# Attention plus rational feed-forward on one core: in the first part's units ScalarE forms the numerator's first step ahead of the absolute value

## The chip, the core and the metric

The program runs on one core of one Trainium2 chip, in float32 from end to end. The metric is the device time of one execution in microseconds (us). The kernel before was run three times: 1244.38, 1244.65 and 1247.54 us, so the median is 1244.65. The engines are named as the profile names them: PE (TensorE's matmuls), PEld (its weight loads), ACT (ScalarE), DVE (VectorE), POOL (GpSimd) and SP (SyncE, whose queue issues most DMAs).

## The reference

Block-causal attention, then a feed-forward layer with a rational function between its two products:

```
scores = (q @ k.T) / 8, masked by 64 x 64 blocks        # 8 x 8 heads, 576 tokens, head size 64
x = softmax(scores) @ v                                  # 4608 x 512
h = x @ w_in                                             # 4608 x 2048
P = a0 + a1*h + a2*h*h + a3*h*h*h
Q = 1 + |b0|*|h| + |b1|*h*h
out = (P / (Q + 1e-6)) @ w_out                           # 4608 x 512
```

## The kernel before

**Attention** runs over 32 pairs of heads, p0 to p31. For each pair, PE makes transposes of q and k (`tp`), scores (`s`), transposes of the exponentials (`t`) and the product with v (`o31_0`, `o31_1` for pair 31). ACT makes the exponentials (L560) and the high halves of split numbers (`ptrh`, `xh`), DVE the maxima (L548) and the low halves (`ptrl`, L612), POOL scales the exponentials (L572). The result goes to the DRAM scratch `xscr`.

**The feed-forward layer** needs each float32 product as three passes over high and low halves. It has two parts. Part 0 (`ph == 0`) covers the first 10 of 16 blocks of the hidden size for 14 chunks of 256 tokens. It runs between the attention pairs, and fills PE's time there. Part 1 covers what is left, after the attention, in chunks of 512 tokens. A unit of part 0 is two hidden blocks by 256 tokens, five units a chunk, 70 in all. A tile's name gives part, chunk and unit: `h0_10_1` is the hidden tile of part 0, chunk 10, unit 1. Its steps are:

- `first`: 24 matmuls of 256 columns make `h` in PSUM (L229). Then ACT reads `h` for `u = |h|` (L236) and for `s = a3*h + a2` (L238), and makes `v = b1*u + b0` (L239). POOL makes `u = v*u` (L243). DVE makes `s = s*h` (L244) and `s = (s + a1)*h` (L245), which also read `h` in PSUM.
- `recip`: ACT makes Ln (L251), Exp (L258) and `s + a0` (L259). DVE makes `gh` (L260) and a correction (L261), POOL the remainder (L263).
- `split`: POOL makes `gl`, the low half (L275).
- `second`: 12 matmuls of 512 columns take `gh` and `gl` with `w_out` (L299). The passes over `gh` can start before `gl` is there.

There is one PSUM tile for `h` in part 0, so the next unit's first matmul waits for L245 of this unit. `u`, `v` and `s` have two buffers each.

**The order on the engines** is not the order of the code. The lines name the work and its dependences, and a scheduler places the instructions by its own estimate of when each could run (`schedule_with_timeline_sim=True`, in the launch code). So moving one line can move others, on every engine. Part 0's units come into the code's order a step at a time between attention steps, by a fixed table of goals, which the change does not touch.

Of the kernel before, what the change touches and what calls it, by code (L numbers as in the profile page):

```python
# [12 lines left out]
AF = mybir.ActivationFunctionType  # L13
# [60 lines left out]
def attn_ffn_kernel(  # L74
# [11 lines left out]
    nc = tc.nc  # L86
# [97 lines left out]
    class Ffn:  # L184
# [34 lines left out]
        def first(self, ph, c, u):  # L219
            xs = self.x[ph, c]  # L220
            tag = f"{ph}_{c}_{u}"
            pool = self.pools[self.n % len(self.pools)]
            hp = self.hpools[self.n % len(self.hpools)]
            h = hp.tile([128, NBU[ph], CTS[ph]], F32, name=f"h{tag}", tag="a", bufs=1 if hp is ps_h else 3)
            for j in range(NBU[ph]):
                w, f = self.block(ph, c, NBU[ph] * u + j)
                for dc in range(4):
                    for i, (y, hl) in enumerate(((0, 1), (0, 0), (1, 0))):
                        nc.tensor.matmul(h[:, j, :], lhsT=w.win(f, dc, y), rhs=xs[dc][:, hl, :],  # L229
                                         start=(dc == 0 and i == 0), stop=(dc == 3 and i == 2))  # L230
            self.n += 1
            hf = h.rearrange("p j t -> p (j t)")
            ut = pool.tile([128, 512], F32, name=f"u{tag}", tag="u", bufs=CBUFS if pool is ffn else 2)
            vt = pool.tile([128, 512], F32, name=f"v{tag}", tag="v", bufs=CBUFS if pool is ffn else 2)
            st = pool.tile([128, 512], F32, name=f"s{tag}", tag="s", bufs=CBUFS if pool is ffn else 2)
            nc.scalar.activation(out=ut, in_=hf, func=AF.Abs)  # L236
            if ph == 0:
                nc.scalar.activation(out=st, in_=hf, func=AF.Identity, scale=a3, bias=a2)  # L238
                nc.scalar.activation(out=vt, in_=ut, func=AF.Identity, scale=b1, bias=b0)  # L239
            else:  # L240
                nc.scalar.activation(out=st, in_=hf, func=AF.Identity, scale=na3, bias=na2)  # L241
                nc.gpsimd.tensor_scalar(out=vt, in0=ut, scalar1=b1, scalar2=b0, op0=ALU.mult, op1=ALU.add)  # L242
            nc.gpsimd.tensor_tensor(out=ut, in0=vt, in1=ut, op=ALU.mult)  # L243
            nc.vector.tensor_tensor(out=st, in0=st, in1=hf, op=ALU.mult)  # L244
            nc.vector.scalar_tensor_tensor(out=st, in0=st, scalar=a1, in1=hf,  # L245
                                           op0=ALU.add if ph == 0 else ALU.subtract, op1=ALU.mult)
            self.m[ph, c, u] = (pool, ut, vt, st)
# [114 lines left out]
    with ExitStack() as actx:  # L362
# [61 lines left out]
        def behind(ins, first):  # L424
            tc.add_manual_dep(ins.ins, first.ins.name,
                              mybir.DependencyInfo(mybir.DependencyClass.NoSync, mybir.DependencyReason.DATA),
                              reason="order")
# [367 lines left out]
```

## Time and profile before

| what | us |
|---|---|
| three runs, median | 1244.65 |
| the profiled execution, its own time | 1246.05 |
| its span in the trace | 1244.3 |
| PE busy in the span | 1191.3 |
| DVE, ACT, POOL busy in the span | 921.3, 908.5, 876.7 |
| the stretch 100 to 850 us (attention and part 0 together): PE busy | 721.85 of 750 |
| the stretch 850 to 1244 us (part 1 alone): PE busy | 388.92 of 394 |

The profiled execution took 1.4 us more than the median, and 1.75 us of its time lie outside the span. A window's row gives each engine's busy time in a stretch. What is missing from the stretch is that engine's idle time. The wait rows then say what PE waited for. Matmuls overlap, so the distance from one start to the next, and not a matmul's own length, is what it costs PE.

### The profile page before, as it was taken

What the parts mean: (1) busy time and instruction counts of PE and PEld (TensorE: products, weight loads), DVE (VectorE), ACT (ScalarE), POOL (GpSimd) and SP (SyncE); (2) the same over time, 40 slices, a digit from 0 to 9 for tenths busy, and PEclk for the clock granted to TensorE, in tenths of its full rate; (3) what the DMA queues carried; (4) which work ended last, traced back from release to release, by engine and by line L of the source; (5) the groups of instructions that cost most, each with busy time, mean ns of one, the idle gap of its engine ahead of it and who ended that gap; (6) DMA issues with size and microseconds to landing.
All of it is one profiled execution on the core that took longest, in us unless ns stands there. A gap on an engine that the chain in (4) does not pass through costs nothing.

```text
span 1244.3 us, 21931 instructions
## 1 busy us (share of the span) xinstructions
PE 1191.3 (96%) x7124; PEld 1008.8 (81%) x7124; DVE 921.3 (74%) x2016; ACT 908.5 (73%) x2025; POOL 876.7 (70%) x1043
## 2 busy tenths in 40 slices
PE   6888999999999999999999999999999999999998
PEld 4666888888888878888888888878888888888886
DVE  6878888777888777877777777647666766677764
ACT  6877888877988878888888888756555655555554
POOL 4666778877888877787777877756665656665664
PEclk8999999999999999999999999999999999999999
DMA  8782344463544545443333342444014344443100
GB/s 233 208 232 71 94 138 113 121 179 89 143 114 132 132 125 143 108 136 100 100 103 92 105 110 68 113 154 189 1 64 131 120 136 136 136 136 102 43 1 34
DMA packets 199506, 145.67 MB, mean 117 GB/s; under 512 B 136288, under 2 KB 164960, under 8 KB 199392
## 3 DMA queue, kind: packets, MB, share of 16 engines
q1 hardware_dynamic: 196624, 143.15, 40.1%
q10 hardware_dynamic: 2704, 1.11, 0.3%
q8 instruction: 57, 0.93, 0.3%
q14 instruction: 57, 0.47, 0.1%
q0 software_dynamic: 64, 0.00, 0.0%
HBM read 92.28 MB, written 41.94 MB: 108 GB/s over the span
## 4 chain that ended last, share of the span: by engine, by line
PE 71%; ACT 8%; POOL 7%; DVE 5%; DMA 5%; issue 3%; SPq 1%; POOLq 0%; ACTq 0%; DVEq 0%
PE h L229 28%; PE o L299 26%; PE o L664 5%; PE t L598 4%; PE s L530 4%; ACT p L560 2%; PE o L625 2%; POOL gl L275 2%; DMA xt<-xh 1%; POOL u L263 1%; PE tp L438 1%; POOL p L572 1%; PE s L513 1%; DMA wri<-in_moe_w_in_dram 1%; DMA x<-xscr 1%
## 5 line engine op out<-in xcount | busy, mean ns | idle before, releaser
L229 PE MATMUL h<-x,wpi 128*128 128x256 f32 (+1 forms) x2568 | 453.6, 324 | 7.2 <-DMA x<-xscr 2.5
L229 PEld LDWEIGHTS h<-x,wpi 128*128 128x128 f32 x2568 | 380.7, 190 | 53.0 <-issue 6.0
L299 PE MATMUL o<-wpo,gh 128*128 128x512 f32 x1152 | 343.8, 395 | 0.0
L299 PEld LDWEIGHTS o<-wpo,gh 128*128 128x128 f32 x1152 | 212.8, 188 | 43.3 <-issue 0.7
L299 PE MATMUL o<-wpo,gl 128*128 128x512 f32 x576 | 210.3, 400 | 8.6 <-POOL gl L275 8.2
L572 POOL TENSOR_SCALAR p<-p,rc 128x128 f32<-128x128 f32 (+4 forms) x288 | 176.1, 623 | 48.4 <-DVE rc L569 32.9
L243 POOL TENSOR_TENSOR u<-v,u 128x512 f32<-128x512 f32 x144 | 187.5, 1302 | 13.2 <-ACT v L239 5.4
L560 ACT ACTIVATE p<-s,nm 128x288 f32<-128x288 f32 (+4 forms) x320 | 168.3, 534 | 25.2 <-DVE nm L548 19.9
L251 ACT ACTIVATE v<-u,qcb 128x512 f32<-128x512 f32 x144 | 105.1, 730 | 82.0 <-POOL u L243 81.7
L244 DVE TENSOR_TENSOR s<-s,h 128x512 f32<-128x512 f32 x144 | 98.5, 684 | 86.4 <-ACT s L241 65.2
L236 ACT ACTIVATE u<-h 128x512 f32<-128x512 f32 x144 | 86.4, 600 | 102.3 <-PE h L229 96.2
L548 DVE TENSOR_REDUCE nm<-s 128x1 f32<-128x128 f32 (+4 forms) x288 | 129.4, 474 | 7.4 <-PE s L513 4.7
L278 POOL TENSOR_TENSOR gl<-s,gh 128x512 fp32r<-128x512 f32 x74 | 95.8, 1294 | 55.0 <-ACT gh L277 54.9
L598 PE MATMUL t<-ident,p 128*128 128x128 f32 x800 | 122.5, 279 | 8.6 <-POOL p L572 4.1
L299 PEld LDWEIGHTS o<-wpo,gl 128*128 128x128 f32 x576 | 104.7, 189 | 31.1 <-POOL gl L275 12.4
L611 ACT CAST ptrh<-t 128x512 fp32r<-128x512 f32 (+1 forms) x189 | 98.4, 542 | 36.9 <-PE t L598 36.6
L612 DVE TENSOR_TENSOR ptrl<-t,ptrh 128x512 fp32r<-128x512 f32 (+1 forms) x189 | 115.5, 627 | 11.5 <-ACT ptrh L611 10.4
L242 POOL TENSOR_SCALAR v<-u,bab 128x512 f32<-128x512 f32 x74 | 57.2, 774 | 91.0 <-ACT u L236 90.9
L598 PEld LDWEIGHTS t<-ident,p 128*128 128x128 f32 x800 | 91.0, 141 | 27.8 <-POOL p L572 6.8
L263 POOL TENSOR_TENSOR u<-s,u 128x512 f32<-128x512 f32 x70 | 90.3, 1290 | 30.3 <-DVE u L261 16.2
L245 DVE SCALAR_TENSOR_TENSOR s<-s,coef,h 128x512 f32<-128x512 f32 x144 | 106.2, 738 | 2.4
L530 PE MATMUL s<-k,q 64*128 64x512 f32 (+3 forms) x768 | 86.4, 343 | 6.6 <-ACT p L560 2.9
(110 smaller groups left out, 2031.5 us busy)
## 6 DMA issues: line engine op xcount, KB each, us to landing
x<-xscr SPq DMA_DIRECT2D x44, 256.0 KB, 4.0
xscr<-xl SPq DMA_DIRECT2D x32, 288.0 KB, 2.4
out_dram<-os SPq DMA_DIRECT2D x34, 256.0 KB, 3.3
qr<-in_q_dram SPq DMA_DIRECT2D x64, 128.0 KB, 2.8
kr<-in_k_dram SPq DMA_DIRECT2D x62, 128.0 KB, 2.5
xt<-xh SPq DMA_DIRECT2D x54, 144.0 KB, 2.3
xscr<-xh SPq DMA_DIRECT2D x54, 144.0 KB, 2.5
pscr<-os SPq DMA_DIRECT2D x14, 512.0 KB, 2.7
```

The source lines that it names most:

```text
L229: nc.tensor.matmul(h[:, j, :], lhsT=w.win(f, dc, y), rhs=xs[dc][:, hl, :], start=(dc == 0 and i == 0), stop=(dc == 3 and i == 2))
L243: nc.gpsimd.tensor_tensor(out=ut, in0=vt, in1=ut, op=ALU.mult)
L245: nc.vector.scalar_tensor_tensor(out=st, in0=st, scalar=a1, in1=hf, op0=ALU.add if ph == 0 else ALU.subtract, op1=ALU.mult)
L251: nc.scalar.activation(out=vt, in_=ut, func=AF.Ln, bias=qcb)
L263: nc.gpsimd.tensor_tensor(out=ut, in0=st, in1=ut, op=ALU.subtract)
L299: nc.tensor.matmul(self.o[m], lhsT=g[:, j, ms], rhs=w.wout(f, y), start=(u == 0 and j == 0 and i == 0), stop=(u == nu - 1 and j == NBU[ph] ...
L530: mm = nc.tensor.matmul(s["s", t, h], lhsT=q[hs, x, 128 * t:128 * t + 128], rhs=k[hs, y, 0:128 * (t + 1)], start=(n == 0 and t == i), stop ...
L548: nc.vector.reduce_max(out=nm[:, j:j + 1], in_=s[d, j][:, :w] if i == 4 else s["s", i, j], axis=AX.X, negate=True)
L560: nc.scalar.activation(out=dst, in_=s.pop((d, j2))[:, :w] if i == 4 else s.pop(("s", i, j2)), func=AF.Exp, bias=nm[:, n:n + 1], scale=1.0, ...
L572: nc.gpsimd.tensor_scalar(out=x, in0=x, scalar1=rc[:, j2:j2 + 1], scalar2=1.0, op0=ALU.mult, op1=ALU.mult)
L598: nc.tensor.transpose(ps[:, 128 * x:128 * x + 128], src[:, 128 * kb:128 * kb + 128], ident)
L612: nc.vector.tensor_tensor(out=dl, in0=src, in1=dh.bitcast(F32), op=ALU.subtract)
```

## The change

In part 0, ACT now makes `s` from `h` first and `u = |h|` after it, then `v` as before. In part 1 nothing moves. No operation is added or taken away, and no shape or buffer changes.

```diff
-            nc.scalar.activation(out=ut, in_=hf, func=AF.Abs)
+            if ph:
+                nc.scalar.activation(out=ut, in_=hf, func=AF.Abs)
             if ph == 0:
                 nc.scalar.activation(out=st, in_=hf, func=AF.Identity, scale=a3, bias=a2)
+                nc.scalar.activation(out=ut, in_=hf, func=AF.Abs)
                 nc.scalar.activation(out=vt, in_=ut, func=AF.Identity, scale=b1, bias=b0)
```

In the changed kernel the three ACT lines are L239 (`s`), L240 (`u`) and L241 (`v`), and every line behind them is two higher (L299 is L301).

In the built programs, the wait of DVE's product (L244, then L246) on ACT is for L238 in all 70 units before, and for L240 in all 70 units now. Each is the second of ACT's two reads of `h`. So the product waits for both reads in either program.

The scheduler's order differs on all engines from the first unit of part 0 to the last. PE's order is the same up to unit 0_0_0's second products, and again from the last attention pair's end on, that is for all of part 1.

**ACT, unit 0_3_1.** Before, from its absolute value on; `p` are exponentials of attention, `ptrh` high halves of transposes:

```order
L236 ACTIVATE u0_3_1_4301<-h0_3_1_4276 128x512
L238 ACTIVATE s0_3_1_4303<-h0_3_1_4276,coef_97 128x512
L560 ACTIVATE p1_124,sm11_4_3605<-s11_4_1_3607,nm11_4_3604 128x256
L560 ACTIVATE p1_124,sm11_4_3605<-s11_4_0_3606,nm11_4_3604 128x256
L239 ACTIVATE v0_3_1_4302<-u0_3_1_4301,bab_102 128x512
L611 CAST ptrh_1534<-t11_1_0_3652 128x4x128
L611 CAST ptrh_1534<-t11_1_1_3659 128x4x128
```

The same unit now, from its first ACT operation on:

```order
L239 ACTIVATE s0_3_1_4303<-h0_3_1_4276,coef_97 128x512
L240 ACTIVATE u0_3_1_4301<-h0_3_1_4276 128x512
L562 ACTIVATE p3_126,sm12_1_3749<-s12_1_1_3751,nm12_1_3748 128x512
L562 ACTIVATE p3_126,sm12_1_3749<-s12_1_0_3750,nm12_1_3748 128x512
L613 CAST ptrh_1534<-t11_3_0_3786 128x2x2x128
L241 ACTIVATE v0_3_1_4302<-u0_3_1_4301,bab_102 128x512
```

`s` and `u` have changed places, `v` stands one row further behind the first of them, and the unit as a whole stands later beside the attention (pair 12's exponentials, no longer pair 11's). Over the 70 units, `v` stands 2.7 rows behind the first operation before and 3.5 now, and the Exp 11.6 and 11.8 rows. An Abs is followed at once by its own `v` in 4 units before and in 23 now, a Ln by its own Exp in 12 and in 22.

**PE, unit 0_3_1's second products.** Before, from pair 13's transposes to unit 0_3_1's first pass over `gl`:

```order
L438 MATMUL tp13_0_3795<-ident_92,qr13_3674 128x128 x4
L299 MATMUL o0_3_0_4679<-wpo0_2_0_1161,gh0_3_1_4509 128x512 x2
L299 MATMUL o0_3_1_4680<-wpo0_2_0_1161,gh0_3_1_4509 128x512 x2
L299 MATMUL o0_3_0_4679<-wpo0_2_0_1161,gl0_3_1_4510 128x512
L530 MATMUL s12_2_1_3813<-k12_3413,q12_3412 128x384
```

The same place now, from behind its passes over `gh` on:

```order
L229 MATMUL h0_3_3_4586<-x0_3_0_4001,wpi0_6_0_1349 128x256 x6
L229 MATMUL h0_3_3_4586<-x0_3_1_4004,wpi0_6_2_1377 128x256 x5
L532 MATMUL s12_4_1_3990<-k12_3413,q12_3412 128x256
L532 MATMUL s12_4_0_3989<-k12_3413,q12_3412 128x256
L532 MATMUL s12_4_1_3990<-k12_3413,q12_3412 128x256
L532 MATMUL s12_4_0_3989<-k12_3413,q12_3412 128x256
L532 MATMUL s12_4_1_3990<-k12_3413,q12_3412 128x256
L532 MATMUL s12_4_0_3989<-k12_3413,q12_3412 128x256
L229 MATMUL h0_3_3_4586<-x0_3_1_4004,wpi0_6_2_1377 128x256
L229 MATMUL h0_3_3_4586<-x0_3_0_4001,wpi0_6_0_1349 128x256 x6
L229 MATMUL h0_3_3_4586<-x0_3_1_4004,wpi0_6_2_1377 128x256 x6
L301 MATMUL o0_3_0_4679<-wpo0_2_0_1161,gl0_3_1_4510 128x512
```

Unit 0_3_3's whole first product and a set of scores now stand between the passes over `gh` and the pass over `gl`, where nothing stood before.

**PE, the end of unit 0_10_1's first product.** Before, from its last rows to the scores of pair 26 (`o0_9_0` and `o0_9_1` are second products of chunk 9):

```order
L229 MATMUL h0_10_1_9539<-x0_10_1_9230,wpi0_2_2_1133 128x256 x4
L299 MATMUL o0_9_0_9175<-wpo0_8_0_1594,gl0_9_4_9484 128x512
L299 MATMUL o0_9_1_9176<-wpo0_8_0_1594,gl0_9_4_9484 128x512
L299 MATMUL o0_9_0_9175<-wpo0_9_0_1621,gh0_9_4_9483 128x512 x2
L598 MATMUL t25_1_1_9158<-ident_92,p3_126 128x128 x4
L513 MATMUL s26_0_0_9210<-k26_8907,qtl0_121 128x288 x3
L299 MATMUL o0_9_0_9175<-wpo0_9_0_1621,gl0_9_4_9484 128x512
L299 MATMUL o0_9_1_9176<-wpo0_9_0_1621,gh0_9_4_9483 128x512 x2
L299 MATMUL o0_9_1_9176<-wpo0_9_0_1621,gl0_9_4_9484 128x512
```

Now, from the same tile's last rows on:

```order
L600 MATMUL t25_1_1_9158<-ident_92,p3_126 128x128 x4
L515 MATMUL s26_0_0_9210<-k26_8907,qtl0_121 128x288 x3
L229 MATMUL h0_10_1_9539<-x0_10_1_9230,wpi0_2_2_1133 128x256 x3
L301 MATMUL o0_9_1_9176<-wpo0_9_0_1621,gh0_9_4_9483 128x512
L301 MATMUL o0_9_1_9176<-wpo0_9_0_1621,gl0_9_4_9484 128x512
L301 MATMUL o0_10_0_9912<-wpo0_0_0_736,gh0_10_0_9612 128x512 x2
```

Six of chunk 9's eight second products, four transposes and three score matmuls stand ahead of the first product's end now; before they stood behind it.

At the end of the attention, four second products of unit 0_13_1 that stood ahead of pair 31's last product with v stand behind it now.

## Rows read from the trace of the kernel before

**Rows 1.** The page's first part: busy time of each engine, its share of the span, and instructions.

```profile
PE 1191.3 (96%) x7124; PEld 1008.8 (81%) x7124; DVE 921.3 (74%) x2016; ACT 908.5 (73%) x2025; POOL 876.7 (70%) x1043
```

**Rows 2.** Windows of the span: from:to and length in us, then busy us (and instructions) of PE, PEld, DVE, ACT and POOL, the granted TensorE clock as a share of full speed, the DMA share and GB/s. The whole stretch of attention and part 0, the stretch of part 1, a 100 us piece of part 1, then twelve pieces of 50 us.

```profile
100.00:850.00 750.00, 721.85 (x4930) 627.65 (x4927) 583.69 (x1408) 612.92 (x1457) 580.49 (x717) 1.00 0.44 120
850.00:1244.00 394.00, 388.92 (x1716) 321.70 (x1714) 263.87 (x389) 220.01 (x359) 238.53 (x214) 1.00 0.26 86
900.00:1000.00 100.00, 100.00 (x443) 82.81 (x442) 68.45 (x103) 57.92 (x95) 61.35 (x55) 1.00 0.33 108
200.00:250.00 50.00, 49.78 (x344) 43.19 (x343) 37.83 (x94) 42.26 (x100) 40.25 (x50) 1.00 0.42 112
250.00:300.00 50.00, 45.94 (x311) 39.66 (x310) 38.45 (x96) 39.26 (x97) 36.71 (x46) 0.97 0.47 130
300.00:350.00 50.00, 49.56 (x349) 43.20 (x349) 42.17 (x102) 44.27 (x106) 40.16 (x52) 1.00 0.50 137
350.00:400.00 50.00, 48.38 (x348) 42.82 (x347) 40.99 (x104) 42.92 (x103) 41.43 (x50) 1.00 0.51 137
400.00:450.00 50.00, 47.57 (x320) 41.50 (x320) 39.75 (x93) 39.16 (x94) 39.80 (x50) 0.97 0.45 125
450.00:500.00 50.00, 47.55 (x333) 40.67 (x331) 38.99 (x99) 41.12 (x103) 39.14 (x49) 1.00 0.47 127
500.00:550.00 50.00, 48.62 (x340) 42.79 (x338) 42.32 (x104) 43.55 (x106) 39.08 (x49) 1.00 0.46 128
550.00:600.00 50.00, 47.60 (x331) 42.09 (x332) 37.65 (x92) 40.25 (x96) 40.30 (x49) 1.00 0.41 106
600.00:650.00 50.00, 49.86 (x351) 43.70 (x351) 38.84 (x97) 40.52 (x100) 39.08 (x49) 1.00 0.38 96
650.00:700.00 50.00, 49.19 (x349) 43.47 (x348) 37.22 (x96) 41.70 (x102) 38.51 (x51) 1.00 0.41 105
700.00:750.00 50.00, 50.00 (x347) 44.11 (x346) 38.27 (x96) 43.11 (x103) 38.58 (x49) 1.00 0.38 104
750.00:800.00 50.00, 49.19 (x344) 42.90 (x342) 35.66 (x92) 38.64 (x92) 37.62 (x48) 1.00 0.34 92
```

**Rows 3.** What PE waited for between 100 and 850 us: us in total, times, longest us.

```profile
PE o L299 <- POOL gl L275: 8.2, 11, 1.8
PE o L648 <- DVE ptrl L612: 2.3, 2, 1.6
PE h L229 <- DVE s L245: 2.2, 4, 1.0
...
PE h L229 <- DVE rc L569: 1.6, 1, 1.6
```

**Rows 4.** ACT and DVE in order of time at unit 0_0_1: start us, length us, instruction, and the idle time before it with what ended it. Then two ACT rows at 337 us, a Ln and the Exp that needs it.

```profile
123.92 0.60 ACT L236 ACTIVATE u<-h 128x512 f32<-128x512 f32 x1 [0.94 <-PE h L229]
124.41 0.77 ACT L238 ACTIVATE s<-h,coef 128x512 f32<-128x512 f32 x1
125.08 0.81 ACT L239 ACTIVATE v<-u,bab 128x512 f32<-128x512 f32 x1
...
125.22 0.69 DVE L244 TENSOR_TENSOR s<-s,h 128x512 f32<-128x512 f32 x1 [1.69 <-ACT s L238]
...
337.08 0.72 ACT L251 ACTIVATE v<-u,qcb 128x512 f32<-128x512 f32 x1
337.83 0.63 ACT L258 ACTIVATE v<-v 128x512 f32<-128x512 f32 x1
```

**Rows 5.** PE and POOL in order of time around unit 0_3_1's `gl`, then three windows there.

```profile
276.88 0.62 PE L229 MATMUL h<-x,wpi 128*128 128x256 f32 x3
...
288.61 1.27 POOL L275 TENSOR_TENSOR gl<-u,v 128x512 fp32r<-128x512 f32 x1
...
289.93 0.49 PE L299 MATMUL o<-wpo,gl 128*128 128x512 f32 x1 [1.79 <-POOL gl L275]
...
288.00:291.00 3.00, 1.21 (x12) 0.83 (x11) 3.00 (x6) 3.00 (x8) 2.92 (x3) 1.00 0.38 87
291.00:294.40 3.40, 3.40 (x15) 2.60 (x12) 2.81 (x9) 2.51 (x6) 1.86 (x4) 0.50 0.01 2
294.40:298.00 3.60, 3.60 (x31) 3.50 (x30) 3.60 (x10) 3.28 (x12) 2.48 (x4) 1.00 0.17 38
```

**Rows 6.** Two windows at 440 us.

```profile
437.70:441.10 3.40, 1.85 (x14) 1.11 (x11) 2.81 (x9) 3.40 (x9) 3.15 (x5) 1.00 0.00 0
441.10:444.60 3.50, 3.50 (x19) 3.50 (x18) 3.46 (x10) 3.50 (x10) 1.64 (x4) 0.51 0.49 176
```

**Rows 7.** PE and POOL in order of time for unit 0_10_1: the end of its first product, its `gl` made, its first passes over `gl`. The row at 546 us is a run of 14 matmuls of 256 columns, and the one behind it starts where the run ends.

```profile
648.67 0.72 PE L229 MATMUL h<-x,wpi 128*128 128x256 f32 x4
...
661.81 1.28 POOL L275 TENSOR_TENSOR gl<-u,v 128x512 fp32r<-128x512 f32 x1
...
664.29 0.72 PE L299 MATMUL o<-wpo,gl 128*128 128x512 f32 x2
...
546.10 1.83 PE L229 MATMUL h<-x,wpi 128*128 128x256 f32 x14
547.77 0.60 PE L598 MATMUL t<-ident,p 128*128 128x128 f32 x4
```

**Rows 8.** PE where part 1's first product goes on, behind the end of the attention.

```profile
837.61 0.70 PE L229 MATMUL h<-x,wpi 128*128 128x512 f32 x2 [1.36 <-DMA x<-xscr]
```

## The prediction

> **What bounds the kernel now.** I read the page's shares first, then the windows, then what PE waited for, and then single places in order of time. PE is busy for 1191.3 of 1244.3 us, and no other engine for more than 921.3 [rows 1]. The windows split the span in two [rows 2]. From 850 us on, in part 1, 443 matmuls of 512 columns fill 100 us with no idle time: one each 0.226 us, at a granted clock of 1.00. That part is as fast as its matmuls. Between 100 and 850 us, where part 0 runs between the attention's pairs, PE is idle for 750 - 721.85 = 28.15 us. This is all that an order can win there, short of the smaller gaps that the windows count as busy. PE's longest waits there are for `gl` from POOL: 8.2 us in 11 times. Behind them come 2.3, 2.2 and a row of still smaller ones, of many kinds [rows 3]. So the kernel is bound by PE, and its losses are many short waits, none on one place alone.
>
> A long wait has a second price. After the 1.79 us that PE waits for `gl` at 288 to 290 us, the granted clock is 0.50 (1.2 in place of 2.4 GHz) for 3.4 us, with 15 matmuls in 3.4 us, and behind that 31 in 3.6 us at 1.00 [rows 5]. At 437.7 to 441.1 us PE is idle for 3.40 - 1.85 = 1.55 us, and the clock then is 0.51 for 3.5 us [rows 6]. Each such stretch loses about half of itself, 1.7 us. Shorter waits are followed by no such stretch: pieces with 2.4 us of idle time in all stay at 1.00 [rows 2].
>
> **The change, part by part.** Part 1 keeps its order: 0 us.
>
> *The first product's chain.* The words of the change suggest that DVE's product `s*h` starts earlier, by one Abs. It doesn't, since the built program has it wait for the second of ACT's two reads of `h`, whichever that is. In the trace the Abs starts at 123.92, the Identity for `s` at 124.41, and DVE's product at 125.22, which is 1.30 us after the first of the two [rows 4]. Now the Identity comes first. Its follower starts 125.08 - 124.41 = 0.67 us after it, the Abs takes 0.60, and DVE starts some 0.04 later as before: 1.31 us. So the PSUM tile of `h` is free no earlier, and the 2.2 us for which PE waits on L245 [rows 3] stay: 0 us.
>
> The trace shows no kernel in which a product starts after the Identity alone. The Trainium skill's page "PSUM — Partial Sum Buffer", section "PSUM bank collisions raise a hardware error", says that the compiler's scheduler orders any two instructions of different engines that touch one bank and quadrant, reads of ACT and DVE included. That is a rule against a gain from this change, and the built waits agree with it. Without it the product would start some 0.6 us earlier, and the 2.2 us could go, by which the time would be 1242.4.
>
> *ACT's own time.* The three operations keep their lengths. But two neighbours on ACT that don't need each other overlap: 0.60 long, 0.49 from start to start. Where the second needs the first, as the Exp the Ln, it starts 0.03 us after its end [rows 4]. The difference is 0.14 us. Now 23 - 4 = 19 more units have the Abs straight ahead of its `v`, and 22 - 12 = 10 more a Ln straight ahead of its Exp. So ACT is held for 29 x 0.14 = 4.1 us more, against 750 - 612.92 = 137 us of idle time in the stretch [rows 2]. The cover is large: 0 us on the path. Without it, the 4.1 us would be the price.
>
> *When `gl` is made.* Chain: `v` is later by the 0.14 and by the 0.8 rows that it stands further back. One ACT instruction holds its queue for 612.92 / 1457 = 0.42 us on the average [rows 2], so together some 0.5 us. The Exp, which `gh` and so `gl` need, is only 0.2 rows further back: 0.1 us, or 0.2 with its own dependence. I take 0.3, between the ends 0.1 and 0.5. Way: I priced PE's rows between a unit's last first product and its first pass over `gl`, for all 70 units, at 0.226 us for 512 columns and (547.77 - 546.10) / 14 = 0.119 for 256 [rows 2, 7], the other shapes in proportion. This estimate gives 14.3 us as the mean before and 14.5 now, so 0.2 of the 0.3 is given back. The 11 waits for `gl` [rows 3] grow by 11 x 0.1 = 1.1 us. This is the middle of a wide interval, because single places move far more than the mean. Two of them:
>
> - Unit 0_3_1: its first product ends at 276.88 + 3 x 0.119 = 277.24, its `gl` is made at 288.61 + 1.27 = 289.88, and PE stood there from 288.14 on [rows 5]. Now 24 matmuls of 256 columns, 24 x 0.119 = 2.9 us, lie between. This wait of 1.79 us should go, and the 1.7 us of slow clock behind it too.
> - Unit 0_10_1: its first product ends at 648.67 + 4 x 0.119 = 649.15, `gl` is made at 663.09, and PE comes for it at 664.29, with 1.2 us to spare [rows 7]. Now six matmuls of 512 columns and seven short ones have moved to the other side: 6 x 0.226 + 7 x 0.119 = 2.2 us. PE comes 1.0 us too early.
>
> Bounds of the term: if all waits for `gl` go, -8.2. If each unit's `gl` came as long after its first product as before, while PE came by the new order, 16 units would wait for 18.7 us in all by the same estimate, which is 18.7 - 8.2 = +10.5. I don't take that end. A unit whose passes the scheduler puts earlier is mostly one whose chain it sees end earlier.
>
> *The attention's end.* PE waits 1.36 us for part 1's inputs at 837.61 [rows 8], which come from the last pair's output. Four second products, 4 x 0.226 = 0.9 us, now stand behind that pair. This fills 0.9 of the wait: -0.9 us, between 0 and -1.36.
>
> *The rest of the order.* Transposes, scores and second products change places all over the stretch, and SP's loads with them. The PE waits other than for `gl` have no reason to grow or to shrink: the same instructions, the same lengths, another draw. What a draw is worth is to be read from the windows. PE's idle time in the twelve pieces from 200 to 800 us is 16.8 us, from 0.00 to 4.06, with a mean of 1.40 and a standard deviation of 1.24 us. For 15 such pieces a draw strays by 1.24 x 3.9 = 4.8 us. To that come the stretches at half clock. There are two now, and none to four would be -3.4 to +3.4 us.
>
> Sum: 0 + 0 + 0 + 1.1 - 0.9 + 0 = +0.2 us. The profiled execution took 1246.05, with 1.75 us outside its span, and it would become 1246.25. It is 1.4 above the median, so the median to expect is 1244.65 + 0.2, about 1244.9.
>
> **The rivals.**
> - *Faster, chance 0.23.* The long waits of the old order go and the new one has only short ones, so that the clock stays at 1.00. For it: the place at 288 us gets 2.9 us of cover, and ten of the fifteen units that PE caught without `gl` have a longer way now. Price: 1.79 + 1.55 us of waits and 2 x 1.7 of clock, 6.7 us, which gives 1238. Against it: a new order has long waits of its own. It decides from the point at which no new wait reaches about 1.5 us.
> - *Slower, chance 0.31.* `gl` becomes a wait at places like unit 0_10_1. By the estimate eleven units that had time to spare lose more of their way than they had, and a later `v` adds up to 0.5 us to each. Price: half of the +10.5, 5.3 us, and one stretch more at half clock, 1.7: 7 us, which gives 1251.7. It decides once `gl` comes later than PE by more than 8.2 us in sum. Against it: the mean way has grown.
> - *The change doesn't do what it says*, in that DVE starts no earlier. That is what I expect, and the forecast has it in it. If DVE did start by 0.6 us earlier, the price is the 2.2 us above, and it would still be within 0.3%.
>
> **How the numbers follow.** The forecast, no difference, is the likeliest: 0.46. A measurement of this kernel can tell about 0.3% from no change, 3.7 us, so "within" is 1240.9 to 1248.4. The draw's 4.8 us and some 1.7 for the clock make 5.1 us; 8 times in 10 is 1.28 x 5.1 = 6.5 us to each side, 1238.4 to 1251.4. To take in more of the bounds of the `gl` term, of which the one above is the further, I widen it to 1237 to 1255. Faster by over 0.3% has 0.23, slower by over 0.3% 0.31: the sum of chain and waits leans a little to the slow side.
>
> **What would show it right or wrong.** In the profile after: part 1 still 443 matmuls in 100 us; DVE's product released by the Abs (L240) and starting 1.3 us after the Identity's start; no wait for `gl` and no half clock after unit 0_3_1; a wait of about 1 us for `gl` at unit 0_10_1; waits for `gl` of 7 to 12 us in all; the idle time of PE between 100 and 850 us within some 5 us of 28.15; a wait of some 0.5 us for part 1's inputs. It would be wrong if idle time moved by more than the draw, or if the waits for attention's tiles (`p`, `ptrl`) moved with a sign of their own, for which I have found no reason.

## The result, and the profile after

The new kernel takes 1259.4 us (median of four runs, 1257.93 to 1259.92), the kernel before 1244.99 on the same chip (1244.38 to 1247.54). The ratio is 1.0094, interval 1.0072 to 1.0117: slower by 14.4 us. The prediction had 1244.9 and a range up to 1255. The profiled execution took 1259.8, its span is 1258.0, 13.7 more than before. Line numbers behind L236 are two higher than before: `s` is L239, `u` L240, `gl` L277, the exponentials L562.

The page's first part answers to [rows 1], the windows to [rows 2]:

```profile
PE 1196.4 (95%) x7124; PEld 1010.9 (80%) x7124; DVE 930.8 (74%) x2016; ACT 910.0 (72%) x2025; POOL 871.6 (69%) x1043
```

```profile
100.00:850.00 750.00, 713.77 (x4897) 620.78 (x4898) 585.34 (x1399) 606.81 (x1446) 566.76 (x711) 1.00 0.42 114
900.00:1000.00 100.00, 100.00 (x443) 82.77 (x443) 67.66 (x101) 57.72 (x95) 61.12 (x56) 1.00 0.30 98
200.00:250.00 50.00, 46.56 (x329) 40.77 (x328) 38.70 (x102) 42.47 (x104) 38.28 (x51) 1.00 0.46 126
250.00:300.00 50.00, 49.00 (x338) 42.63 (x338) 40.21 (x97) 41.87 (x103) 40.79 (x52) 1.00 0.46 128
300.00:350.00 50.00, 46.84 (x329) 40.67 (x328) 40.25 (x95) 40.24 (x100) 35.85 (x45) 1.00 0.47 124
350.00:400.00 50.00, 45.56 (x318) 39.22 (x318) 40.94 (x97) 39.44 (x94) 39.34 (x48) 1.00 0.50 138
400.00:450.00 50.00, 46.25 (x311) 40.09 (x311) 38.36 (x92) 39.41 (x97) 38.99 (x51) 1.00 0.40 104
700.00:750.00 50.00, 50.00 (x352) 44.26 (x351) 39.35 (x95) 41.51 (x100) 39.53 (x50) 1.00 0.39 102
```

Part 1 is untouched: 443 matmuls in 100 us. Between 100 and 850 us PE is idle for 750 - 713.77 = 36.23 us, 8.1 more than before. The pieces at 200, 350 and 300 us have lost most, 3.2, 2.8 and 2.7 us, while the one at 250 us is fuller than before and the one at 700 us as full.

To split the 13.7 us, two windows were laid over the same work: from part 0's first matmul to a point early in part 1. Both hold 4966 matmuls. The first row is of the kernel before, the second of the new one:

```profile
91.00:843.00 752.00, 723.11 (x4966) 629.01 (x4963) 582.20 (x1416) 613.88 (x1467) 578.87 (x720) 1.00 0.43 118
```

```profile
94.40:856.70 762.30, 725.02 (x4966) 629.64 (x4963) 592.16 (x1416) 615.35 (x1466) 573.87 (x720) 1.00 0.42 116
```

The stretch starts 3.4 us later and is 10.3 us longer. Of the 10.3, (762.30 - 725.02) - (752.00 - 723.11) = 8.4 are idle time, and 1.9 lie within what counts as busy. The 3.4 us ahead of it are not the change: PE's order is the same up to there. The new profile has stretches at half clock in the start-up, two of which are these:

```profile
66.40:69.80 3.40, 3.40 (x5) 1.54 (x6) 2.92 (x12) 2.79 (x11) 1.71 (x4) 0.50 0.53 166
86.90:90.30 3.40, 3.40 (x7) 1.70 (x7) 1.52 (x7) 1.42 (x5) 2.57 (x5) 0.50 0.97 284
```

In the 18 profiles of the experiments part 0's first matmul starts anywhere from 90.92 to 93.08 us: with the new order at 91.06 (e9) and at 93.08 (e5), with the old one at 91.04 (e16) and at 92.78 (e10). One profile's difference thus holds a few us of chance. The 14.4 us are the difference of two medians of four runs, and don't rest on one profile.

What PE waited for between 100 and 850 us, answering to [rows 3]:

```profile
PE o L301 <- POOL gl L277: 13.6, 17, 1.8
PE s L532 <- ACT p L562: 6.2, 7, 2.0
PE h L229 <- DVE s L247: 3.4, 5, 1.3
```

`gl` has grown from 8.2 to 13.6 us. The waits for `p`, ACT's exponentials (a score's PSUM tile is free once they are made), are now second with 6.2. Before, their row was this, below the rows shown:

```profile
PE s L530 <- ACT p L560: 0.7, 2, 0.4
```

ACT itself waits in the same stretch of the new kernel:

```profile
ACT p L562 <- DVE nm L550: 24.7, 20, 5.5
ACT s L239 <- POOL u L265: 13.4, 8, 2.9
```

The second row has no counterpart before, and the first had 17.4 us. `s` has two buffers, so a unit's first step on ACT waits until POOL's remainder has read the `s` of the unit two before. One such place, PE, ACT and POOL in order of time:

```profile
461.92 2.13 POOL L574 TENSOR_SCALAR p<-p,rc 128x384 f32<-128x384 f32 x2 [1.10 <-DVE k L423]
462.64 0.96 DVE L263 SCALAR_TENSOR_TENSOR u<-u,gh 128x512 f32<-128x512 f32 x1
...
464.02 1.28 POOL L178 TENSOR_TENSOR wpi<-wai,wbi 128x512 fp32r<-128x512 f32 x1
...
465.69 1.28 POOL L265 TENSOR_TENSOR u<-s,u 128x512 f32<-128x512 f32 x1
...
467.00 0.78 ACT L239 ACTIVATE s<-h,coef 128x512 f32<-128x512 f32 x1 [1.60 <-POOL u L265]
467.63 1.27 POOL L277 TENSOR_TENSOR gl<-u,v 128x512 fp32r<-128x512 f32 x1
467.68 0.59 ACT L240 ACTIVATE u<-h 128x512 f32<-128x512 f32 x1
468.16 0.58 ACT L668 CAST xh<-o 128x512 fp32r<-128x512 f32 x1
468.37 0.69 DVE L246 TENSOR_TENSOR s<-s,h 128x512 f32<-128x512 f32 x1 [1.85 <-ACT u L240]
...
468.95 1.03 PE L301 MATMUL o<-wpo,gl 128*128 128x512 f32 x2 [1.75 <-POOL gl L277]
```

DVE has the correction ready at 462.64 + 0.96 = 463.60, but POOL is at a scaling of `p` and at a weight conversion, and comes to the remainder 2.1 us later. ACT stands 1.60 us for the buffer, with the attention's cast of `xh` behind it in its queue. DVE stands 1.85 behind ACT, and PE 1.75 for `gl`. After that the clock is at its lower level:

```profile
469.20:472.60 3.40, 3.40 (x10) 2.50 (x10) 2.95 (x7) 2.26 (x6) 3.40 (x4) 0.50 0.63 142
```

So ACT, DVE and PE all stand in one place, behind POOL's queue. The page's chain of work that ended last points the same way for the whole span, in shares by engine. First the kernel before, then the new one:

```profile
PE 71%; ACT 8%; POOL 7%; DVE 5%; DMA 5%; issue 3%; SPq 1%; POOLq 0%; ACTq 0%; DVEq 0%
```

```profile
PE 60%; ACT 11%; DVE 11%; POOL 10%; issue 4%; DMA 3%; SPq 0%; POOLq 0%; ACTq 0%; DVEq 0%
```

### The profile page after: what moved, and what is told of

Read it like the earlier page. It is cut to its first block, busy times and chain, and to the rows that moved or that the text cites. A ratio compares the mean times of both kernels' runs of the same rounds, so it can differ in the third digit from the quotient of the medians.

```text
span 1258.0 us, 21946 instructions
## 1 busy us (share of the span) xinstructions
PE 1196.4 (95%) x7124; PEld 1010.9 (80%) x7124; DVE 930.8 (74%) x2016; ACT 910.0 (72%) x2025; POOL 871.6 (69%) x1043
## 4 chain that ended last, share of the span: by engine, by line
PE 60%; ACT 11%; DVE 11%; POOL 10%; issue 4%; DMA 3%; SPq 0%; POOLq 0%; ACTq 0%; DVEq 0%
PE h L229 24%; PE o L301 22%; PE o L666 4%; ACT p L562 3%; PE s L532 3%; PE t L600 2%; POOL gl L277 2%; PE o L627 2%; POOL p L574 2%; POOL u L265 2%; DVE u L263 1%; DVE nm L550 1%; DVE ptrl L614 1%; DVE gh L262 1%; ACT ptrh L613 1%
## 5 line engine op out<-in xcount | busy, mean ns | idle before, releaser
L301 PE MATMUL o<-wpo,gh 128*128 128x512 f32 x1152 | 341.7, 394 | 0.7 <-DVE gh L262 0.7
L301 PEld LDWEIGHTS o<-wpo,gh 128*128 128x128 f32 x1152 | 212.8, 188 | 45.0 <-DVE gh L262 1.5
L301 PE MATMUL o<-wpo,gl 128*128 128x512 f32 x576 | 210.0, 401 | 14.6 <-POOL gl L277 14.6
L245 POOL TENSOR_TENSOR u<-v,u 128x512 f32<-128x512 f32 x144 | 186.7, 1296 | 18.6 <-ACT v L241 11.2
L562 ACT ACTIVATE p<-s,nm 128x288 f32<-128x288 f32 (+4 forms) x320 | 168.5, 534 | 32.6 <-DVE nm L550 27.7
L246 DVE TENSOR_TENSOR s<-s,h 128x512 f32<-128x512 f32 x144 | 98.5, 684 | 93.9 <-ACT s L243 63.4
L301 PEld LDWEIGHTS o<-wpo,gl 128*128 128x128 f32 x576 | 104.2, 189 | 38.6 <-POOL gl L277 19.1
L244 POOL TENSOR_SCALAR v<-u,bab 128x512 f32<-128x512 f32 x74 | 57.1, 771 | 89.4 <-ACT u L237 89.2
L265 POOL TENSOR_TENSOR u<-s,u 128x512 f32<-128x512 f32 x70 | 90.7, 1296 | 40.5 <-DVE u L263 30.9
L237 ACT ACTIVATE u<-h 128x512 f32<-128x512 f32 x74 | 44.1, 596 | 75.9 <-PE h L229 75.4
```

Of the source, the lines that this page charges most:

```text
L265: nc.gpsimd.tensor_tensor(out=ut, in0=st, in1=ut, op=ALU.subtract)
L301: nc.tensor.matmul(self.o[m], lhsT=g[:, j, ms], rhs=w.wout(f, y), start=(u == 0 and j == 0 and i == 0), stop=(u == nu - 1 and j == NBU[ph] ...
L562: nc.scalar.activation(out=dst, in_=s.pop((d, j2))[:, :w] if i == 4 else s.pop(("s", i, j2)), func=AF.Exp, bias=nm[:, n:n + 1], scale=1.0, ...
```

## The experiments

Two kinds of edits were used: the code edited for some units only, which lets the scheduler make another order; and the scheduled program edited, which keeps every engine's order. Times are medians beside those of the kernel before in the same batch, since batches differ by some us.

### Is it the exchange, or the order?

**e1** takes the old program and exchanges the two reads of `h` on ACT in 62 units, each in place; `L` is the list of scheduled instructions.

```diff
         attn_ffn_kernel(tc, *args)
+    exchange(nc, (236, 238, 239), lambda unit: True)
...
+            L[k1] = _remake(b, [*a.sync_info.on_wait, *b.sync_info.on_wait], a.sync_info.on_update)
+            L[k2] = _remake(a, [], b.sync_info.on_update)
```

> The program before, with every engine's order as it was, and only ACT's two reads of h exchanged in 62 of the 70 units of part 0 (the 8 units where v stood between them are left). v waits for the Abs, DVE's product for the second read, as in the changed kernel. Theory A (the loss is the scheduler's new order, the exchange itself costs nothing): within 0.3% of before, 1241 to 1249 us, waits of PE for gl of 8 to 10 us. Theory B (the exchange itself makes v and gl late, and PE waits): most of the +14 us, 1254 to 1260, waits for gl of about 14 us.

Measured: 1250.08 against 1246.57, ratio 1.0029 (1.0013 to 1.0046), 1 us above theory A's range and 4 below theory B's. PE's wait for `gl` stays near the 8.2 us of before:

```profile
PE o L299 <- POOL gl L275: 8.7, 12, 1.4
```

In the old order the exchange itself so costs some 3.5 us, which is at the edge of what can be told from no change; the interval allows up to 0.5%.

**e5** does the reverse in the new program: the same helper exchanges the two reads back in all 70 units, and nothing else moves.

```diff
+    n = exchange(nc, (239, 240, 241))
```

> The new kernel's program with ACT's two reads of h exchanged back in place in all 70 units: every engine keeps the new order, row for row, only Abs and Identity stand the old way round. Theory A (the loss is the new order on the other engines; the exchange itself costs nothing): as slow as the new kernel, 1256 to 1262 us, ratio 1.008 to 1.013. Theory B (the exchange makes v, and so gl, late): v is 0.5 to 0.6 us earlier again in each unit, and most of the loss comes back, 1245 to 1250. If only part of the waits for gl (14.6 us) hangs on v: between the two, with the waits for gl falling by as much as the time.

Measured: 1263.62 against 1246.09, ratio 1.0133 (1.0113 to 1.0153), just above theory A's range. The loss stays in full with the exchange undone. It is the order of the rows on the engines, as theory A said; theory B falls.

### How far does such an order stray?

Six kernels make the exchange in some units only:

```diff
-            nc.scalar.activation(out=ut, in_=hf, func=AF.Abs)
+            second = ph == 0 and (c, u) == (0, 0)
+            if not second:
+                nc.scalar.activation(out=ut, in_=hf, func=AF.Abs)
             if ph == 0:
                 nc.scalar.activation(out=st, in_=hf, func=AF.Identity, scale=a3, bias=a2)
+                if second:
+                    nc.scalar.activation(out=ut, in_=hf, func=AF.Abs)
```

Here it is unit 0_0_0 alone (e2); the others have `c < 3` (e3), `c >= 3` (e4), unit 0_7_0 (e8), unit 0_10_1 (e17) and `3 <= c < 8` (e18) in the condition.

> Only unit 0_0_0, one of 70, has its Identity ahead of its Abs; the scheduler plans anew from there on, and its order differs nearly as widely as in the changed kernel. Theory A: the time is another draw, as likely above as below the changed kernel's, and more than 4 us away from before more likely than not (1240 to 1262). Theory B: one seventieth of the loss, 1245 to 1246 us.

> Only the 15 units of chunks 0 to 2 are changed; the new order differs from before in a third as many rows as the changed kernel's and comes together with it again and again later on. Theory A: a loss only where the order differs, up to some 5 us, so 1241 to 1251, and no loss between 300 and 560 us if the order there is before's. Theory B: 15 of 70 units, +3 us, about 1248.

> Only the 55 units of chunks 3 to 13 are changed; the first 260 us keep before's order. Theory A: another draw from there on, 1241 to 1258, its loss not in the proportion of the units and not needed between 300 and 560 us. Theory B: 55 of 70 units, +11 us, 1254 to 1258, most of it as waits for gl between 300 and 560 us as in the changed kernel.

> Only unit 0_7_0 has its two reads exchanged in the code; the order differs from PE's row 1645 on, in 401 rows of difference, so nothing before some 480 us moves. Theory A, order as a draw: a change of either sign, within about 5 us of 1244.7; if the old order is a favourable one, more likely slower than faster. Theory B: one unit's v by 0.5 us, no measurable change, 1244.7 within 0.3%.

> Only unit 0_10_1 is exchanged in the code; the order differs from PE's row 2238 on, late in part 0, in 625 rows of difference. If the old order is a favourable one, so that most others are slower: 1247 to 1255. If draws stray to both sides by 5 us about the old one: 1240 to 1250, as likely below as above.

> The units of chunks 3 to 7 are exchanged; the order differs from PE's row 858 on, in 1288 rows. If the old order is a favourable one: 1249 to 1262, between the eleven chunks' 1260.7 and the three chunks' 1249.1. If draws stray to both sides: 1240 to 1250.

The second column counts the lines of a diff between PE's order before and now, where equal matmuls in a row are one line.

| exchanged in the code | lines of difference on PE | time, before in the batch | ratio, interval |
|---|---|---|---|
| all 70 units (the change) | 1677 | 1259.4, 1244.99 | 1.0094, 1.0072 to 1.0117 |
| e2: unit 0_0_0 | 1914 | 1254.54, 1246.57 | 1.0063, 1.0044 to 1.0083 |
| e4: chunks 3 to 13 | 1426 | 1260.65, 1246.57 | 1.0112, 1.0089 to 1.0135 |
| e18: chunks 3 to 7 | 1288 | 1256.45, 1247.42 | 1.0072, 1.0048 to 1.0096 |
| e17: unit 0_10_1 | 625 | 1245.2, 1247.42 | 0.9981, 0.9965 to 0.9998 |
| e3: chunks 0 to 2 | 595 | 1249.13, 1246.57 | 1.0021, 1.0008 to 1.0034 |
| e8: unit 0_7_0 | 401 | 1249.85, 1246.09 | 1.0026, 1.0009 to 1.0043 |

One unit of 70 costs 8 us, over half of the whole change, and gives 1914 lines of difference on PE. Four of the seven orders are slower by more than the 0.3% that can be told, e3 and e8 by less, and e17 lies about as far on the other side. The mean ratio is 1.0053 (6.6 us). The four with over 1000 lines are the four slowest, though among them the loss doesn't follow the count. So the old order is a favourable one among these, and what led far away from it lost. Two expectations were missed: e4 came out above both of its ranges, and e17 fell into the range for draws to both sides, below the one for a favourable order. The seven orders share units and are not independent draws; that they are enough to put a number on the next one isn't shown.

### Which waits make the new order slow?

**e6** and **e7** take the waits for `gl` away, in the new and in the old program: part 0's third pass reads `w_out` as its weights in place of `gl`, so the low half's share of the output is left out.

```diff
+            g = mb.PhysicalAccessPattern(ap=[list(w.ap[0]), [1, 128]], offset=w.offset, dtype=w.dtype, memref=w.memref,
+                                         memsetref=w.memsetref)
+            L[k] = again(i, [w, g], [x for x in s.on_wait if not x.ant_name.startswith("Pool")] if s else [],
+                         list(s.on_update) if s else [], 0)
```

> The new kernel's program, every engine in the same order, but part 0's third pass takes its weights from w_out in place of gl, so that PE waits for gl nowhere in part 0 (the low half's share of the output is left out; 280 matmuls keep their size and place, and the transposes that were covered by a wait for gl have their own wait for POOL). If the waits for gl (14.6 us in 18 times, and the half clock behind the long ones) are the loss: 1259.4 - 14.6 = 1244.8 or somewhat less. If they only stand in for other waits (for p, for s, for h), which then take their place: above 1250, with those waits grown.

> The same on the kernel before, which waits 8.2 us for gl in 11 times and has two stretches of half clock behind long waits: 1244.7 - 8.2 - up to 3.4 = 1233 to 1237 if these waits are all lost time; above 1240 if others take their place. The difference to the new order without gl is what the new order loses by other waits: 14.4 - 6.4 = 8 us if the waits for gl account for 6.4 us of it; some 2 us if they account, with the clock, for all but the early part.

Measured: 1254.95 (new) and 1240.69 (old), with 1246.09 before; ratios 1.0074 (1.0059 to 1.0089) and 0.996 (0.9941 to 0.998). The difference between the orders is 14.3 us, as without the edit. So the waits for `gl`, the largest row by far and the one that grew most, are not the loss. From 90 to 870 us the new order waits 14.6 us for `gl`:

```profile
PE o L301 <- POOL gl L277: 14.6, 18, 1.8
```

It got 4.5 us back, or 2.5 by the ratios. Others took their place, as e6's waits of PE in that stretch show:

```profile
PE s L532 <- ACT p L562: 8.2, 8, 2.0
PE h L229 <- DVE s L247: 5.8, 7, 1.9
PE s L532 <- DVE ptrl L614: 3.5, 4, 1.7
```

In the new kernel these three had 6.2, 3.4 and 1.5. My account by wait rows had failed, and theory C took its place: the new order ties PE to the three other engines' queues as a whole.

**e9** to **e16** test it. In the scheduled program, the operations of a unit that work in place keep 64 of 512 columns: all eight of them (e9 new, e10 old), ACT's three (e11 new, e15 old), DVE's three (e12 new, e14 old), POOL's two (e13 new, e16 old). The other columns are left out. `cut` is applied to the operands:

```diff
+        return mb.PhysicalAccessPattern(ap=[list(x.ap[0]), [1, columns]], offset=x.offset, dtype=x.dtype, memref=x.memref,
+                                        memsetref=x.memsetref)
...
+    n = narrow(nc, (253, 260, 261, 246, 247, 263, 245, 265))
```

> The new kernel's program, every engine in the same order, but the eight operations of part 0's units that work in place (ACT: Ln, Exp, s + a0; DVE: s*h, (s + a1)*h, the correction; POOL: v*u and the remainder) keep 64 of 512 columns in all 70 units; the rest of the columns goes on unfinished, so that part of the feed-forward is left out. In the trace after, the chain that ended last runs 60% through PE and 32% through ACT, DVE and POOL, against 71% and 20% before. Theory C (the new order leaves PE tied to the queues of the three other engines, whose unit work delays both gl and the attention's tiles): with short unit work nearly all of the difference goes, 1228 to 1238 us, within 4 us of the old order with the same cut. Theory D (PE's own order against the attention's round trips, and the clock, lose the time): the new order keeps 8 to 14 us over the old one with the same cut.

> The same cut on the kernel before: 1244.7 less its waits for gl, for s and the like, 1228 to 1238 us in either theory. What counts is the difference to the new order with the same cut: under 4 us by theory C, 8 to 14 by theory D.

> The new kernel's program in the same order with ACT's three in-place operations of a unit alone (Ln, Exp, s + a0) at 64 of 512 columns; the rest of their columns is left out. If the tie is to ACT's queue, which the waits for p (6.2 us against 0.7 before) point to: these waits fall below 2 us and the time to 1250 or less. If it is to DVE or POOL: 1253 to 1260.

> The kernel before with ACT's three in-place operations of a unit at 64 of 512 columns, against the new order with the same cut, 1248.8 us. If ACT's queue is the tie: 1244 to 1250, hardly any gain by the cut. If not: 1234 to 1241.

> The same with DVE's three in-place operations of a unit alone (s*h, (s + a1)*h, the correction). If the tie is to DVE, whose share of the chain that ended last rose most, from 5% to 11%: 1250 or less, with the waits for h and ptrl gone. If it is to ACT: 1253 to 1260.

> The kernel before with DVE's three in-place operations of a unit at 64 of 512 columns, against the new order with the same cut, 1238.1 us. If DVE's queue is what the new order is tied to: within 4 us of that, 1234 to 1242. If not: 1223 to 1231, since the old order would gain as much by the cut.

> The new kernel's program in the same order with POOL's two in-place operations of a unit alone (v*u and the remainder) at 64 of 512 columns; the rest of their columns is left out. In the trace after, ACT's first step of a unit stands 13.4 us in 8 times, up to 2.9, until POOL's remainder of the unit two before has given back the s buffer; in the trace before there is no such wait. If this wait, with the attention's exponentials behind it, is the tie: 1235 to 1242, and within 4 us of the old order with the same cut. If it isn't, 1242 to 1250, with 8 us or more to the old order with the same cut.

> The kernel before with POOL's two in-place operations of a unit at 64 of 512 columns: what the cut is worth where ACT never waits for POOL's remainder. With the tie at POOL's late return of the buffers: 1235 to 1243, within 4 us of the new order with the same cut; without: 8 to 14 us below the new one.

| what is cut | new order, ratio | old order, ratio | new less old |
|---|---|---|---|
| nothing | 1259.4, 1.0094 | 1244.99, 1 | +14.4 us |
| the reads of `gl`, replaced (e6, e7) | 1254.95, 1.0074 | 1240.69, 0.996 | +14.3 |
| ACT's three (e11, e15) | 1248.81, 1.0004 | 1243.12, 0.997 | +5.7 |
| DVE's three (e12, e14) | 1238.1, 0.9922 | 1238.98, 0.9931 | -0.9 |
| POOL's two (e13, e16) | 1232.79, 0.9893 | 1235.63, 0.9909 | -2.8 |
| all eight (e9, e10) | 1222.72, 0.9808 | 1228.26, 0.9845 | -5.5 |

The rows ACT's three and DVE's three compare two batches, whose kernels before differ by 0.9 us; by the ratios they are +4.2 and -1.1. Against their expectations, e13 came out 2 us below its range and e15 between its two. POOL's remainder, as an example, falls from 1296 to 329 ns, here in the groups by line of the new kernel and of e9:

```profile
L265 POOL TENSOR_TENSOR u<-s,u 128x512 f32<-128x512 f32 x69 | 89.4, 1296 | 37.5 <-DVE u L263 27.8 <-DVE rc L571 6.5 <-DVE s L527 1.9
```

```profile
L265 POOL TENSOR_TENSOR u<-s,u 128x64 f32<-128x64 f32 x70 | 23.0, 329 | 24.2 <-DVE u L263 19.4 <-DVE rc L571 2.2 <-DVE s L527 0.9
```

With short unit work the new order is the faster one, by 5.5 us. Theory D, which kept it 8 to 14 us slower, falls, and PE's own rows in it are no worse. Theory C has the direction; the time of e9 and the 5.5 us lie beyond what it allowed, on the side away from D. Cutting DVE's share alone, or POOL's alone, takes away the whole difference, and ACT's some 60 to 70% of it. The loss is thus no property of one queue: it hangs on the unit work of all three. Why that is so is in part argued. A unit's chain runs through all three queues, and a shorter operation both shortens that chain and frees its queue for the attention's work sooner; no run tells the two apart. The share of PE in the chain that ended last rises with the cut: e9 has it at 86%, e10 at 84%.

```profile
PE 86%; ACT 5%; DVE 3%; DMA 2%; issue 1%; POOL 1%; SPq 1%; ACTq 0%; POOLq 0%; DVEq 0%
```

ACT's wait for the `s` buffer can't be the whole of it. In e13 (first row) it falls from 13.4 to 0.9 us, and the difference is gone; but in e12 (second row) it is still there, and the difference is gone too:

```profile
ACT s L239 <- POOL u L265: 0.9, 2, 0.7
```

```profile
ACT s L239 <- POOL u L265: 9.4, 8, 2.4
```

Nor are PE's waits for `p`, the row that grew by 5.5 us. With ACT's three cut they were expected to fall below 2 us; e11 has 5.6. And where the difference is gone they are only 1.0 to 1.5 us smaller than the 6.2 of the new kernel. Here are e9, e12 and e13:

```profile
PE s L532 <- ACT p L562: 4.7, 5, 2.0
```

```profile
PE s L532 <- ACT p L562: 5.2, 6, 1.9
```

```profile
PE s L532 <- ACT p L562: 4.8, 5, 2.0
```

A third buffer for `s` would test the wait by itself, but SBUF has no room for one beside the other tiles, so it wasn't tried. Which rows of which queue use up the slack stays open. No version that beats the kernel before came out of this: e17, at 0.9981, lies within the 0.3%.

## Why the prediction was wrong

*What held.* Part 1 kept its 443 matmuls in 100 us [rows 2]. DVE's product `s*h` is released by the Abs, and at the place shown above it starts 468.37 - 467.00 = 1.37 us after the Identity, where 1.3 was forecast [rows 4]. The wait behind unit 0_3_1 [rows 5] is gone, with its half clock: `gl` is made at 299.36, PE comes for it at 303.56 without a wait, and the pieces from 250 to 350 us are at 1.00. Unit 0_10_1 [rows 7] waits 0.69 us where the estimate had 1.0. ACT's own time is not the loss: e1 exchanges 62 units for 1.0029, and e5 won nothing by undoing 70.

The rows for `gl`, POOL's and PE's in order of time, for unit 0_3_1 and then PE's for unit 0_10_1:

```profile
298.07 1.29 POOL L277 TENSOR_TENSOR gl<-u,v 128x512 fp32r<-128x512 f32 x1
...
303.56 0.62 PE L301 MATMUL o<-wpo,gl 128*128 128x512 f32 x2
...
680.12 0.73 PE L301 MATMUL o<-wpo,gl 128*128 128x512 f32 x2 [0.69 <-POOL gl L277]
```

*What failed: "The rest of the order".* That step put the mean of the draw at zero and its spread at 4.8 us, from how PE's idle time varies from window to window within the old order. Such windows tell how one order varies along its way, not how other orders stand to it. The measured orders have their mean at +6.6 us, and this one is at +14.4. PE's idle time between 100 and 850 us rose by 8.1 us, more than the draw. The step also said that waits other than for `gl` "have no reason to grow or to shrink: the same instructions, the same lengths". The runs showed a reason in its place: the same instructions, in the new order, depend on how long the unit work holds the three queues. With that work cut, the +14.4 us become +5.7 (ACT), -0.9 (DVE), -2.8 (POOL) and -5.5 (all eight). The waits for `p`, which the prediction named as what would make it wrong, rose from 0.7 to 6.2 us. They are a sign of the new order and not its loss, since they stay where the difference is gone. Which rows lose the time stays open.

*The term for `gl`* was mis-sized as a row, +1.1 against +5.4 (13.6 less 8.2). That is within the bounds it was given. But e6 and e7 show that a sum of waits was the wrong measure in the first place: with all of them gone, the difference between the orders is unchanged. The rival "Slower" had the sign and 7 of the 14 us. Its mechanism, `gl` as the wait that decides, falls with the same two runs. The third stretch at half clock that it added didn't come in this part of the program: there are two from 100 to 850 us, at 107.4 and 469.2, as there were two before.

*The price of a long wait* was read too simply. The prediction had a stretch at half clock behind the waits of 1.55 and 1.79 us, and took about 1.5 us as the point that decides. The kernel before already has a wait of 1.56 us with no such stretch behind it, and the new one has waits of 2.04 and 1.75 us without one. The first two rows are of the kernel before, the others of the new one:

```profile
266.84 0.30 PE L648 MATMUL o<-ptrh,vst 128*128 128x64 f32 x1 [1.56 <-DVE ptrl L612]
266.84:270.24 3.40, 2.83 (x14) 2.33 (x15) 3.00 (x11) 3.40 (x13) 2.83 (x4) 1.00 0.60 152
```

```profile
125.27 1.08 PE L532 MATMUL s<-k,q 64*128 64x384 f32 x12 [2.04 <-ACT p L562]
357.26 0.74 PE L301 MATMUL o<-wpo,gl 128*128 128x512 f32 x2 [1.75 <-POOL gl L277]
...
125.27:128.67 3.40, 3.40 (x32) 3.26 (x33) 2.88 (x10) 2.26 (x8) 2.60 (x4) 1.00 0.14 32
357.26:360.66 3.40, 3.40 (x21) 2.99 (x22) 3.20 (x10) 3.13 (x9) 3.13 (x4) 1.00 0.54 124
```

This changes no term of the sum, since the number of such stretches came out at two.

*The attention's end* [rows 8] had -0.9 us. At the place where PE waited 1.36 us for a load it now waits for none, but it waits for `gh` and `gl` beside it:

```profile
849.76 1.20 PE L301 MATMUL o<-wpo,gh 128*128 128x512 f32 x4 [0.31 <-DVE gh L262]
850.79 1.57 PE L229 MATMUL h<-x,wpi 128*128 128x512 f32 x6
853.35 0.73 PE L301 MATMUL o<-wpo,gl 128*128 128x512 f32 x2 [0.98 <-POOL gl L277]
```

These are 1.29 us, in place of 1.36, or of 1.76 with one of 0.40 us that stood behind it at 841.46. So at most half of the term came.

*The start-up* was not in the sum. Its 3.4 us are seen in the one profile; whether the three other timed runs of the new kernel have them isn't shown.

## What to carry to other kernels

Where a scheduler sets the order, ask first how many rows an edit moves, and try the edit on one unit: here one exchange of two independent operations in one unit of 70 cost 8 us with next to none of its own time, and orders that led far from a good one were slower four times out of four. Don't add up wait rows of a nearly full engine: removing the largest gave back 2.5 to 4.5 of 14.6 us in the new order and 4.3 to 5.4 of 8.2 in the old one, and told nothing of the difference between them. A row that grew need not be the loss either, as the waits for `p` show. The share of the bound engine in the chain that ended last (71% against 60%) pointed the right way here, but it doesn't rank orders: e4, with the highest ratio of the seven, has 68%, and e3, within 0.3%, has 66%. Editing the scheduled program, with the order held, tells an operation's own cost from that of the order.

## What was not expected of the hardware

The clock in the start-up differs from one execution to the next with the same rows on PE: part 0's first matmul started at 90.92 to 94.53 us over 20 profiles, in three groups some 1.7 us apart (near 91.1, near 92.8, and 94.5). A stretch of 3.4 us at half clock is worth 1.7. The length of one wait doesn't tell whether such a stretch follows: in the new kernel's trace the clock was at 0.50 for 3.4 us after PE's wait of 1.75 us at 468.95, and at 1.00 after one of 1.75 us at 357.26 and one of 2.04 us at 125.27. The stretch at 107.4 us came after two short waits, of 0.54 and 1.04 us with 0.66 us of work between them. What else decides is open. An operation on 64 of 512 columns is far from an eighth of the time: POOL's remainder took 0.33 in place of 1.30 us, ACT's Exp 0.27 in place of 0.64.
